# Negated scores, threshold and bias on ScalarE, and a new order of the list schedule

## The chip, the cores and the metric

One NeuronCore of one Trainium2 chip runs the whole program. The metric is the device time of one execution in microseconds (us), as a median over runs. Engines are named as in the profile: PE (TensorE matmul), PEld (its weight loads), DVE (VectorE), ACT (ScalarE), POOL (GpSimd), SP (SyncE, which only issues DMAs here).

## The reference

Attention with a thresholded softmax, then two feed-forward blocks; the first gates two projections and multiplies by `w3` and `w_out`, the second applies an ELU between `w_in` and `w_out`.

```python
# q, k, v: 4 batches x 8 heads x 576 x 64, tau = 0.02
scores = scale * np.matmul(q, k.transpose(0, 1, 3, 2))
thresh = np.max(scores, axis=-1, keepdims=True) - tau
scores = np.where(scores >= thresh, scores, -1000000000.0)
scores = scores - np.max(scores, axis=-1, keepdims=True)
attn = np.exp(scores)
attn = attn / (np.sum(attn, axis=-1, keepdims=True) + 1e-09)
attn_out = np.matmul(attn, v)
...
a = x @ w1                     # x: 2304 x 512, w1, w2: 512 x 1024
b = x @ w2
x = (a * b @ w3) @ w_out       # w3: 1024 x 1024, w_out: 1024 x 512
...
h = x @ w_in                   # 512 x 2048
g = np.where(h > 0.0, h, alpha * (np.exp(np.minimum(h, 0.0)) - 1.0))
return (g @ w_out).astype(np.float32)
```

## The kernel before

**Stages.** The program has four stages. The first is attention together with the projections `ab` of batches 0 to 2. Then come the `ab` of batch 3, the product M = w3 w_out with its use on g (tiles `m` and `x2`), and the second feed-forward block (tiles `h` and `o`).

**Attention.** The 32 heads are 16 pairs. A pair has 9 score tiles of 128 rows by 576 keys, so there are 144 tiles, numbered i in the order `SEQ`. Each passes through these steps:

- `emit_S` (PE) writes the scores to one of three PSUM buffers `s`.
- `emit_max` (DVE) writes the negated row maximum to column 0 of the small tile `st`.
- `emit_bias` and `emit_tiny` (POOL, lines 423 and 419) make from it the bias of the exponential (column 2) and the threshold (column 1).
- `emit_exp` (ACT) writes the exponentials `e`.
- `emit_mask` (DVE, line 436) compares the scores with the threshold and multiplies.

The masked tile is then transposed in one of two ways. Tiles of the DMA way are split into two fp16 halves by `emit_H` (ACT, line 443) and `emit_L` (POOL, lines 447 and 448) and transposed by `emit_T`, a DMA on SP's queue. The halves lie in one of four buffers `hl`, which is free again when its DMA has read it. Tiles of the other way are transposed on PE by `emit_X` and copied by `emit_C` (ACT, line 488), and keep their PSUM buffer `s` until that copy.

**Plain and split pairs.** Pairs 0 to 3 (`NPL`) are "plain": their 36 tiles come first, their scores are made from fp32 operands, and the softmax scale `esc` is applied in the exponential. Pairs 4 to 15 are "split": `prep_s` (POOL) first scales q by `esc`, then q and k are parted into a high and a low half, so that the scores are already scaled. `by_dma(i)` is true for 10 plain and 84 split tiles. Of split pairs, the first four tiles of pairs 4 to 9 go by PE; the rest goes by DMA.

**After a group of tiles.** A pair's tiles form two groups n (4 and 5 tiles). For each group `emit_rr` (DVE) inverts the row sums, `turn_r` (PE, line 502) and `keep_r` (ACT, line 507) turn them, and `store_r` and `load_rs` (SP) send them through DRAM. `emit_PV` (PE, lines 541 and 549) multiplies with v, `emit_xf` (DVE) normalizes, and `emit_xh` (ACT, line 566) and `emit_xl` (DVE) split the result. The `ab` units of batch b (line 591) need all groups of four pairs; a unit is 12 matmuls and its results leave through `keep_a` (ACT, line 599) or `make_g` (DVE, line 606) and `store_g` (SP, line 610).

**What sets the order.** The first stage is recorded as operations with a cost, an engine and a key, and a list scheduler (`Plan`) sorts them once, when the program is built. On every engine the instructions then run in that fixed order. `AHEAD` shifts the keys by operation and stage, `SLACK` says how far an engine may look past the earliest ready operation, and the numbers in the `op(...)` calls are the assumed durations. The order within later stages is written out by hand. The weights of the third stage are loaded by DMAs from ACT's queue (`load_w`, line 237) and converted by `conv_ops` on ACT, DVE and POOL; the first of these DMAs stands on ACT behind the last instruction of the first stage.

```python
ring["s", i] = take("s", 3, o)
re = take("e", EB, ex)             # EB = 4
rh = take("hl", HLB, hi)           # HLB = 4
```

Of the kernel before, what the change touches and what calls it, by code (L numbers as in the profile page):

```python
# [69 lines left out]

# [1306 lines left out]
```

## Time and profile before

| | us |
|---|---|
| median of 3 runs | 1003.58 |
| lowest and highest run | 1001.97, 1007.71 |
| the profiled execution | 1006.17 |
| its span, first to last instruction | 1004.4 |
| PE busy | 964.4 (96%) |
| DVE busy | 716.5 (71%) |
| POOL busy | 657.6 (65%) |
| ACT busy | 564.2 (56%) |
| mean granted PE clock | 0.993 of full speed |

Busy times are unions of what an engine had in work, over the whole span. Only the first stage, which ends at 419.41 us of the span, is ordered by the scheduler; shares of that stage are read from windows of it.

### The profile page before, as it was taken

To read this page: it belongs to the slowest core of one execution; us is meant where nothing else is said; L and a number is where in the kernel's file an instruction comes from. 1 tells how busy PE (TensorE), PEld (TensorE's weight loads), DVE (VectorE), ACT (ScalarE), POOL (GpSimd) and SP (SyncE) were. 2 spreads that over 40 slices of the span, in tenths; PEclk is the share of its full clock that TensorE was granted. 3 is DMA by queue.
4 is the path that set the end of the run, shared out by engine and by line. 5 is a ranking of instruction groups with operands and counts; after the bars stand their busy time and mean duration, and the time that the engine had idled before them with its cause. 6 is when DMAs were issued, how large, how long until landed. Compare 5 with 4: busy or idle time off the path is not lost. (4 is left out here: it accounts for less than half of the span.)

```text
span 1004.4 us, 18071 instructions
## 1 busy us (share of the span) xinstructions
PE 964.4 (96%) x6102; PEld 846.7 (84%) x6102; DVE 716.5 (71%) x1234; ACT 564.2 (56%) x1045; POOL 657.6 (65%) x849
## 2 busy tenths in 40 slices
PE   8899999989999999999999999999999999999998
PEld 5556788858888888899789999898989999899997
DVE  7887988868776677489775654789676656765563
ACT  5787778768666566355435334645555344553442
POOL 4468787868898999255322223888787576875662
PEclk9999999979999999999999999999999999999999
DMA  8446666577887967777747965731215221141201
GB/s 270 152 127 194 135 147 160 143 163 156 190 185 176 191 159 150 192 259 252 250 152 246 311 228 173 260 116 54 65 51 180 72 69 52 49 132 58 69 22 63
DMA packets 182263, 152.51 MB, mean 152 GB/s; under 512 B 119484, under 2 KB 168860, under 8 KB 177564
## 3 DMA queue, kind: packets, MB, share of 16 engines
q1 hardware_dynamic: 178060, 121.72, 44.8%
q10 hardware_dynamic: 4112, 29.66, 8.4%
q8 instruction: 48, 0.79, 0.3%
q14 instruction: 43, 0.35, 0.1%
HBM read 98.89 MB, written 24.72 MB: 123 GB/s over the span
## 5 line engine op out<-in xcount | busy, mean ns | idle before, releaser
L591 PE MATMUL ab<-x,W 128*128 128x256 f32 (+1 forms) x1536 | 227.4, 298 | 0.8 <-DVE xf L560 0.7
L1206 PE MATMUL o<-W,gg 128*128 128x512 f32 x864 | 222.9, 390 | 0.0
L591 PEld LDWEIGHTS ab<-x,W 128*128 128x128 f32 x1536 | 208.3, 188 | 8.2 <-issue 5.2
L1115 POOL TENSOR_TENSOR wi<-wr,wi 128x256 fp32r<-128x256 f32 x168 | 144.3, 871 | 65.8 <-ACT wi L1114 53.3
L1206 PEld LDWEIGHTS o<-W,gg 128*128 128x128 f32 x864 | 159.9, 188 | 21.5
L436 DVE SCALAR_TENSOR_TENSOR e<-s,st,e 128x576 f32<-128x576 f32 x144 | 115.7, 813 | 31.3 <-ACT e L430 24.8
L1194 POOL TENSOR_TENSOR gg<-th,gg 128x384 fp32r<-128x384 f32 x96 | 106.3, 1108 | 46.5 <-PE h L1246 26.4
L415 DVE TENSOR_REDUCE st<-s 128x1 f32<-128x576 f32 x144 | 107.0, 751 | 27.4 <-PE s L406 12.7
L447 POOL TENSOR_TENSOR hl<-e,hl 128x512 f16<-128x512 f32 x94 | 110.4, 1175 | 19.7 <-ACT hl L443 19.2
L1246 PE MATMUL h<-sl,wi 128*128 128x384 f32 x576 | 116.5, 338 | 2.1 <-DVE th L1276 1.2
L1188 ACT ACTIVATE et<-et 128x384 f32<-128x384 f32 x96 | 50.1, 522 | 111.9 <-DVE et L1187 111.5
L1246 PEld LDWEIGHTS h<-sl,wi 128*128 128x128 f32 x576 | 102.5, 188 | 11.2 <-DVE th L1276 2.0
L1125 PE MATMUL x<-sl,M 128*128 128x384 f32 x576 | 100.6, 336 | 1.4 <-DVE sl L242 1.4
L1125 PEld LDWEIGHTS x<-sl,M 128*128 128x128 f32 x576 | 99.8, 188 | 2.1 <-DVE sl L242 2.0
L1193 ACT ACTIVATE gg<-th 128x384 fp32r<-128x384 f32 x96 | 50.6, 527 | 76.9 <-DVE th L1191 76.5
L1276 DVE TENSOR_TENSOR th<-h,th 128x384 f32<-128x384 f32 x96 | 53.2, 554 | 56.9 <-PE h L1246 56.8
L406 PE MATMUL s<-qk 128*128 128x288 f32 x480 | 86.7, 310 | 7.1 <-DVE e L436 3.7
L430 ACT ACTIVATE e<-s,st 128x576 f32<-128x576 f32 x108 | 77.8, 736 | 27.1 <-POOL st L423 21.5
L1246 PE MATMUL h<-so,wi 128*128 128x384 f32 x432 | 87.5, 337 | 2.6 <-ACT th L1286 1.8
L1246 PEld LDWEIGHTS h<-so,wi 128*128 128x128 f32 x432 | 76.6, 188 | 10.8 <-ACT th L1286 3.9
L406 PEld LDWEIGHTS s<-qk 128*128 128x128 f32 x480 | 69.5, 192 | 17.0 <-issue 6.2
L1191 DVE SCALAR_TENSOR_TENSOR th<-et,th 128x384 f32<-128x384 f32 x96 | 71.6, 746 | 16.8 <-ACT et L1188 15.4
(112 smaller groups left out, 1539.0 us busy)
## 6 DMA issues: line engine op xcount, KB each, us to landing
wr<-wi_dr SPq DMA_DIRECT2D x168, 128.0 KB
rqk<-in_qk SPq DMA_DIRECT2D x24, 576.0 KB
raw_wo<-in_wo ACTq DMA_DIRECT2D x12, 1024.0 KB
th<-g_dr SPq DMA_DIRECT2D x48, 192.0 KB
raw_w<-in_w SPq DMA_DIRECT2D x8, 1024.0 KB
raw_w<-in_w3t ACTq DMA_DIRECT2D x8, 1024.0 KB
raw_win<-in_win ACTq DMA_DIRECT2D x8, 1024.0 KB
vr<-in_v SPq DMA_DIRECT2D x16, 320.0 KB
```

Source lines behind the costliest of these rows:

```text
L406: T.matmul(s[:, n, :HS], q, k[:, c:c + HS], start=(x == 0), stop=(x == len(ops) - 1))
L415: V.tensor_reduce(st[i][:, 0:1], sc[i][:, :, :HS], axis=AX.XY, op=ALU.max, negate=True)
L430: A.activation(et[i], sc[i][:, :, :HS], AF.Exp, bias=st[i][:, 2:3] if by_dma(i) else st[i][:, 0:1])
L436: V.scalar_tensor_tensor(et[i], sc[i][:, :, :HS], st[i][:, 1:2], et[i], op0=ALU.is_ge, op1=ALU.mult, accum_out=sm[p][:, pos:pos + 1],)
L447: G.tensor_tensor(t[:, S + 64:], e[:, :512], t[:, :512], op=ALU.subtract)
L591: T.matmul(o[:, :w], wf[:, m, wx, kt, :], x[:, xx, :], start=(kt == 0 and k == 0), stop=(kt == NK - 1 and k == 2),)
L1115: G.tensor_tensor(t[:, 1], r, f32(t[:, 0]), op=ALU.subtract)
L1125: T.matmul(o[:, :TB], M[:, f, mx, e * P:(e + 1) * P], gh[j, f][:, gx, :], start=(k == 0), stop=(k == 23),)
L1191: V.scalar_tensor_tensor(x, c["t"], -1.0, x, op0=ALU.add, op1=ALU.max)
L1194: G.tensor_tensor(h[:, 1, :], x, f32(h[:, 0, :]), op=ALU.subtract)
L1206: T.matmul(po[j, t], dst["h"][:, gx, t * P:(t + 1) * P], WO[f][:, wx, :], start=(first and k == 0), stop=(last and k == 2),)
L1246: T.matmul(o[:, :TB], w[:, wx, kt, :], bs[k][:, kt, xx, :], start=(i == 0), stop=(i == 5),)
```

## The change

Scores of split pairs are made from q scaled by `nesc` = -`esc`, so they come out negated. The row reduction of a split tile is then a minimum, its result needs no negation, the comparison is `is_le`, and the exponential takes `scale=-1.0`. `lift` holds tau in column 0 and `LNS` in column 1. One ScalarE instruction adds column 0 of `st` to one column of `lift`, or to both, and so writes the threshold and, where the tile goes by DMA, the bias. For plain tiles the two small instructions also move from POOL to ACT. Assumed durations, `SLACK` and the table `AHEAD` get new numbers, so that the whole first stage is ordered anew.

```diff
-SLACK = {"PE": 0, "DVE": 0.08, "ACT": 0.03, "POOL": 0.27, "SP": 0.09, "NEW": 0.05}
+SLACK = {"PE": 0.02, "DVE": 0.06, "ACT": 0.04, "POOL": 0.5, "SP": 0.0, "NEW": 0.05}
 AHEAD = {
-    ("emit_C", 0): 101, ("emit_C", 1): -80.5, ("emit_C", 2): 21, ("emit_H", 1): -14, ("emit_H", 2): 69.5,
...
+    ("emit_C", 0): 59.5, ("emit_C", 1): -139, ("emit_C", 2): -202, ("emit_H", 1): -201.5, ("emit_H", 2): 190.5,
...
     def prep_s(h):
-        G.tensor_scalar(raw[h][:, :S], raw[h][:, :S], esc, 0.0, op0=ALU.mult, op1=ALU.add)
+        G.tensor_scalar(raw[h][:, :S], raw[h][:, :S], nesc, 0.0, op0=ALU.mult, op1=ALU.add)
...
-        V.tensor_reduce(st[i][:, 0:1], sc[i][:, :, :HS], axis=AX.XY, op=ALU.max, negate=True)
+        plain = i < NPL * TPP
+        V.tensor_reduce(st[i][:, 0:1], sc[i][:, :, :HS], axis=AX.XY, op=ALU.max if plain else ALU.min, negate=plain)
+
+    def emit_bias(i):
+        if by_dma(i):
+            A.activation(st[i][:, 2:3], st[i][:, 0:1], AF.Identity, bias=lift[:, 1:2], scale=esc)
+        else:
+            A.activation(st[i][:, 2:3], st[i][:, 0:1], AF.Copy, scale=esc)
 
     def emit_tiny(i):
         t = st[i]
-        G.tensor_scalar(t[:, 1:2], t[:, 0:1], -1.0, add2[:, (k := int(i >= NPL * TPP)):k + 1], op0=ALU.mult, op1=ALU.add)
-
-    def emit_bias(i):
-        t = st[i]
-        G.tensor_scalar(t[:, 2:3], t[:, 0:1], esc if i < NPL * TPP else 1.0, LNS if by_dma(i) else 0.0, op0=ALU.mult, op1=ALU.add)
+        if i < NPL * TPP:
+            A.activation(t[:, 1:2], t[:, 0:1], AF.Identity, bias=drop, scale=-1.0)
+        else:
+            w = 1 + int(by_dma(i))
+            A.activation(t[:, 1:1 + w], lift[:, :w], AF.Identity, bias=t[:, 0:1])
...
-            A.activation(et[i], sc[i][:, :, :HS], AF.Exp, bias=st[i][:, 2:3] if by_dma(i) else st[i][:, 0:1])
+            A.activation(et[i], sc[i][:, :, :HS], AF.Exp, bias=st[i][:, 2:3] if by_dma(i) else st[i][:, 0:1], scale=-1.0)
...
-            op0=ALU.is_ge, op1=ALU.mult, accum_out=sm[p][:, pos:pos + 1],
+            op0=ALU.is_ge if i < NPL * TPP else ALU.is_le, op1=ALU.mult, accum_out=sm[p][:, pos:pos + 1],
...
-        bi = op(call(emit_bias, i), [mx], "POOL", 0.22, i - 10) if plain or by_dma(i) else mx
-        ty = op(call(emit_tiny, i), [mx, bi], "POOL", 0.24, i - 9)
-        ex = op(call(emit_exp, i), [bi], "ACT", 0.715 if plain else 0.625, i)
+        bi = op(call(emit_bias, i), [mx], "ACT", 0.15, i - 10) if plain else mx
+        ty = op(call(emit_tiny, i), [mx], "ACT", 0.15, i - 9)
+        bi = ty if by_dma(i) else bi
+        ex = op(call(emit_exp, i), [bi], "ACT", 0.73 if plain else 0.645, i)
```

**What the order becomes on ACT at the start of the program.** The names are tiles with their numbers: `e0` is the exponential of tile 0, `st0` its small tile, `u_w12` a weight conversion, `pt` the target of `emit_C`. Before:

```order
L428 ACTIVATE e0_179<-s0_155,st0_168,esc_113 128x576
L428 ACTIVATE e1_188<-s1_163,st1_177,esc_113 128x576
L252 ACTIVATE u_w120_201<-raw_w120_148 128x1024
L428 ACTIVATE e2_211<-s2_171,st2_193,esc_113 128x576
L488 ACTIVATE pt0_0_198<-s0_155 128x5x128
```

With the change, the same stretch of ACT:

```order
L429 ACTIVATE st0_171<-st0_171,drop_117 128x1
L424 ACTIVATE st0_171<-st0_171,esc_113 128x1
L437 ACTIVATE e0_182<-s0_158,st0_171,esc_113 128x576
L429 ACTIVATE st1_180<-st1_180,drop_117 128x1
L424 ACTIVATE st1_180<-st1_180,esc_113 128x1
L437 ACTIVATE e1_191<-s1_166,st1_180,esc_113 128x576
L253 ACTIVATE u_w120_204<-raw_w120_151 128x1024
L429 ACTIVATE st2_199<-st2_199,drop_117 128x1
L424 ACTIVATE st2_199<-st2_199,esc_113 128x1
L497 ACTIVATE pt0_0_203<-s0_158 128x5x128
L437 ACTIVATE e2_222<-s2_174,st2_199,esc_113 128x576
```

Each plain tile has two more instructions on ACT, ahead of its exponential. Over the program ACT's rows go from 1062 to 1242 and POOL's from 854 to 590.

**On SP at the end of pair 7**, tiles 67 to 71, the last before a stretch in which no `ab` unit stands on PE. `hl67` to `hl70` are what is transposed, `rd7_1` the row sums that `store_r` sends out, `g0_1_6` a result of `ab`. Before:

```order
L610 DMA g_dr_67<-g0_1_6_2586 128x2x320
L521 DMA rd7_1_2692<-rt7_1_2683 2x128 x2
L522 DMA rd7_1_2692<-rt7_1_2683 2x1x64
L476 DMA_TRANSPOSE pt7_1_2711<-hl67_2513 128x9x128
L476 DMA_TRANSPOSE pt7_1_2711<-hl68_2548 128x9x128
L476 DMA_TRANSPOSE pt7_1_2711<-hl69_2602 128x9x128
L476 DMA_TRANSPOSE pt7_1_2711<-hl70_2650 128x9x128
L527 DMA rb7_1_2774<-rd7_1_2692 64x320 x2
L474 DMA_TRANSPOSE pt7_1_2711<-hl71_2744 128x9x64 x2
```

With the change:

```order
L619 DMA g_dr_67<-g0_1_6_2575 128x2x320
L485 DMA_TRANSPOSE pt7_1_2672<-hl67_2528 128x9x128
L485 DMA_TRANSPOSE pt7_1_2672<-hl68_2549 128x9x128
L485 DMA_TRANSPOSE pt7_1_2672<-hl69_2607 128x9x128
L485 DMA_TRANSPOSE pt7_1_2672<-hl70_2629 128x9x128
L530 DMA rd7_1_2732<-rt7_1_2692 2x128 x2
L531 DMA rd7_1_2732<-rt7_1_2692 2x1x64
L483 DMA_TRANSPOSE pt7_1_2672<-hl71_2709 128x9x64 x2
L536 DMA rb7_1_2768<-rd7_1_2732 64x320 x2
```

The four transposes have moved ahead of the store of the row sums. On PE, score tiles 73 and 74 stand behind the last `ab` unit of batch 0 with the change, and stood ahead of its end before; so ten score tiles (73 to 82) instead of eight (75 to 82) lie between the last `ab` unit of batch 0 and the first of batch 1.

**On ACT at the end of the first stage.** `x15_0` and `x15_1` are the results of the last pair, `a2_0_*` the evictions of the last `ab` units of batch 2, `raw_wo10` the first weight load of the third stage. Before:

```order
L443 ACTIVATE hl143_5720<-e143_5694 128x576
L599 ACTIVATE a2_0_6_5731<-ab2_0_6_0_5700 128x256
L507 ACTIVATE rt15_1_5735<-s145_5699 5x128
L566 ACTIVATE x15_0_5793<-xf15_0_5785 128x256
L599 ACTIVATE a2_0_7_5806<-ab2_0_7_0_5781 128x256
L566 ACTIVATE x15_1_5850<-xf15_1_5848 128x320
L237 DMA raw_wo10_5895<-in_wo1 128x2048
```

With the change:

```order
L452 ACTIVATE hl143_5568<-e143_5537 128x576
L516 ACTIVATE rt15_1_5580<-s145_5559 5x128
L608 ACTIVATE a2_0_4_5598<-ab2_0_4_0_5560 128x256
L575 ACTIVATE x15_0_5636<-xf15_0_5628 128x256
L608 ACTIVATE a2_0_5_5665<-ab2_0_5_0_5643 128x256
L608 ACTIVATE a2_0_6_5698<-ab2_0_6_0_5676 128x256
L575 ACTIVATE x15_1_5734<-xf15_1_5726 128x320
L608 ACTIVATE a2_0_7_5759<-ab2_0_7_0_5740 128x256
L238 DMA raw_wo10_5814<-in_wo1 128x2048
```

More `ab` units of batch 2 now come late: on PE, three whole units (36 matmuls) stand behind the last PV of pair 15 with the change, and none did before; between the last score tile and that PV stand seven units instead of five. The first weight load now stands behind the eviction of a unit that has one more unit after it on PE.

## Rows read from the trace of the kernel before

**Rows 1.** The page, part 1: busy time, share and instructions of each engine.

```profile
PE 964.4 (96%) x6102; PEld 846.7 (84%) x6102; DVE 716.5 (71%) x1234; ACT 564.2 (56%) x1045; POOL 657.6 (65%) x849
```

**Rows 2.** Windows: length, busy us of PE, PEld, DVE, ACT, POOL, clock, DMA.

```profile
8.00:50.00 42.00, 37.63 (x286) 22.97 (x284) 36.68 (x71) 32.88 (x48) 19.50 (x38) 1.00 0.64 209
50.00:199.00 149.00, 144.94 (x1104) 113.45 (x1101) 126.17 (x261) 114.55 (x185) 118.85 (x192) 1.00 0.60 153
199.00:223.00 24.00, 20.62 (x140) 14.29 (x139) 16.92 (x37) 15.64 (x29) 15.14 (x25) 0.79 0.67 142
223.00:300.00 77.00, 73.06 (x574) 64.84 (x573) 59.76 (x127) 53.85 (x93) 66.65 (x116) 1.00 0.80 179
300.00:388.00 88.00, 82.30 (x688) 77.15 (x688) 60.15 (x136) 56.92 (x100) 78.62 (x133) 1.00 0.80 173
388.00:419.41 31.41, 27.85 (x269) 25.19 (x265) 18.79 (x45) 15.44 (x30) 19.07 (x37) 1.00 0.71 146
419.41:470.40 50.99, 50.99 (x384) 50.99 (x385) 41.77 (x45) 25.76 (x36) 23.22 (x9) 1.00 0.77 267
```

**Rows 3.** Groups by line over the span: busy and mean ns, idle before.

```profile
L419 POOL TENSOR_SCALAR st<-st,add 128x1 f32<-128x1 f32 x144 | 44.4, 309 | 14.8 <-DVE st L415 4.5 <-DVE rr L496 0.7 <-PE pv L549 0.4
L423 POOL TENSOR_SCALAR st<-st 128x1 f32<-128x1 f32 x84 | 19.2, 229 | 12.5 <-DVE st L415 5.3 <-ACT hl L443 0.6 <-DVE vst L354 0.2
L423 POOL TENSOR_SCALAR st<-st,esc 128x1 f32<-128x1 f32 x36 | 13.3, 368 | 34.9 <-DVE st L415 33.4 <-ACT e L428 0.3 <-DVE rr L496 0.3
L430 ACT ACTIVATE e<-s,st 128x576 f32<-128x576 f32 x108 | 77.8, 736 | 27.1 <-POOL st L423 21.5 <-DVE st L415 4.2 <-PE s L502 0.9
```

**Rows 4.** Groups by line of ACT, from 8 to 50 us.

```profile
L428 ACT ACTIVATE e<-s,st,esc 128x576 f32<-128x576 f32 x16 | 12.8, 825 | 7.7 <-POOL st L423 7.3
```

**Rows 5.** Timeline of ACT: start, length, instruction, idle before it.

```profile
400.13 0.25 ACT L507 ACTIVATE rt<-s 4x128 f32<-4x128 f32 x1
400.29 1.34 ACT L430 ACTIVATE e<-s,st 128x576 f32<-128x576 f32 x2
```

**Rows 6.** Timelines of DVE, POOL and ACT: the first tile.

```profile
6.82 0.76 DVE L415 TENSOR_REDUCE st<-s 128x1 f32<-128x576 f32 x1 [0.29 <-PE s L394]
...
7.77 0.26 POOL L423 TENSOR_SCALAR st<-st,esc 128x1 f32<-128x1 f32 x1 [5.21 <-DVE st L415]
...
8.07 1.71 ACT L428 ACTIVATE e<-s,st,esc 128x576 f32<-128x576 f32 x2 [5.26 <-POOL st L423]
```

**Rows 7.** Timeline of 196 to 226: SP's issues, ACT and PE.

```profile
200.59 0.38 SPq L610 DMA_DIRECT2D g_dr<-g  x1
...
202.47 6.19 SPq L476 DMA_TRANSPOSE pt<-hl  x4
...
207.00 0.68 ACT L443 ACTIVATE hl<-e 128x576 f16<-128x576 f32 x1 [2.13 <-DMA pt<-hl]
...
208.33 2.82 PE L406 MATMUL s<-qk 128*128 128x288 f32 x12 [1.68 <-ACT pt L488]
```

**Rows 8.** Waits of PE from 206 to 419.41: us in total, times, longest.

```profile
PE s L502 <- DVE st L415: 3.5, 4, 1.7
PE s L406 <- DVE e L436: 3.5, 7, 1.3
```

**Rows 9.** Timeline of PE and ACT: the end of the first stage.

```profile
409.30 0.28 PE L502 MATMUL s<-ident,rr 128*5 128x128 f32 x1 [0.67 <-DVE rr L497]
...
416.05 0.30 PE L549 MATMUL pv<-pt,v 128*64 128x320 f16 x1 [0.74 <-DMA pt<-hl]
...
419.41 51.15 PE L591 MATMUL ab<-x,W 128*128 128x320 f32 x384 [0.74 <-DVE xf L560]
...
419.40 0.83 ACTq L237 DMA_DIRECT2D raw_wo<-in_wo  x2
```

**Rows 10.** Timeline of the third stage: PE waits for an eviction of M.

```profile
494.83 5.56 PE L922 MATMUL m<-WO,w 128*128 128x512 f32 x16 [2.49 <-DVE M L932]
```

**Rows 11.** Timeline of PE around 276: a wait in the middle of the stage.

```profile
276.10 0.27 PE L502 MATMUL s<-ident,rr 128*5 128x128 f32 x1 [1.70 <-DVE st L415]
```

More of the change, by code (lines that the diff above doesn't have):

```diff
@@ new lines @@
+    ("keep_r", 0): -235, ("keep_r", 1): -313.5, ("load_plain", 0): -33.5, ("load_qk", 0): 370, ("load_rs", 0): 129,
+    ("load_rs", 1): -279.5, ("load_v", 0): -3.5, ("load_w", 0): -256.5, ("low", 0): -178, ("new_pt", 0): 145.5,
+    ("prep_h", 0): -492.5, ("prep_lk", 0): 333.5, ("prep_lq", 0): 44, ("prep_s", 0): 57.5, ("prep_v", 0): 294.5,
+    ("prep_vl", 0): 239.5, ("rest", 0): -31.5, ("run_ab", 0): 3, ("run_ab", 1): 2.5, ("run_ab", 2): 3,
+    ("sign", 0): 415.5, ("store_g", 0): -369, ("store_g", 1): -75.5, ("store_g", 2): -209.5, ("store_r", 0): 30,
@@ L69 @@
+    ("store_r", 1): -45, ("top", 0): 186.5, ("turn_r", 0): -149.5, ("turn_r", 1): -18, ("v_mean", 0): -98.5,
+    ("v_scale", 0): -76.5, ("v_sum", 0): 175.5,
 }
@@ L288, in attention_moe_moe2 @@
     tmp1 = cst.tile([P, 1], F32, name="tmp1")
-    add2 = cst.tile([P, 2], F32, name="add2")
+    nesc = cst.tile([P, 1], F32, name="nesc")
+    lift = cst.tile([P, 2], F32, name="lift")
+    drop = cst.tile([P, 1], F32, name="drop")
     ident = hp_.tile([P, P], F32, name="ident")
@@ L388, in emit_S @@
         j, t = ORDER[pos]
-        a, b = qkt[2 * p], qkt[2 * p + 1]
+        a = qkt[2 * p + j % 2]
         if p < NPL:
@@ L627, in attention_moe_moe2 @@
     V.tensor_scalar(tmp1, tau_sb, 0.0, 1e30, op0=ALU.is_lt, op1=ALU.mult)
-    V.tensor_scalar(add2[:, 1:2], tau_sb, 0.0, tmp1, op0=ALU.max, op1=ALU.add)
-    V.tensor_scalar(add2[:, 0:1], add2[:, 1:2], -(D ** 0.5), None, op0=ALU.mult)
-    V.tensor_scalar(add2[:, 1:2], add2[:, 1:2], -1.0, None, op0=ALU.mult)
+    V.tensor_scalar(lift[:, 0:1], tau_sb, 0.0, tmp1, op0=ALU.max, op1=ALU.add)
+    V.memset(lift[:, 1:2], LNS)
+    V.tensor_scalar(drop, lift[:, 0:1], -(D ** 0.5), None, op0=ALU.mult)
+    V.tensor_scalar(nesc, esc, -1.0, None, op0=ALU.mult)
     pl = Plan()
@@ L665, in attention_moe_moe2 @@
         if by_dma(i):
-            hi = op(call(emit_H, i), [mk], "ACT", 0.575, i - 1)
+            hi = op(call(emit_H, i), [mk], "ACT", 0.6, i - 1)
             rh = take("hl", HLB, hi)
-            lo = op(call(emit_L, i), [hi], "POOL", 1.42, i - 1)
+            lo = op(call(emit_L, i), [hi], "POOL", 1.44, i - 1)
             re += [mk, hi, lo]
@@ L672, in attention_moe_moe2 @@
         else:
-            xo = op(call(emit_X, i), [mk], "PE", 0.54, i - 2)
-            co = op(call(emit_C, i), [xo], "ACT", 0.59, i - 3)
+            xo = op(call(emit_X, i), [mk], "PE", 0.61, i - 2)
+            co = op(call(emit_C, i), [xo], "ACT", 0.61, i - 3)
             ring["s", i] += [xo, co]
@@ L710, in attention_moe_moe2 @@
         vh = op(call(prep_v, p), [ve], "ACT", 0.72, t0)
-        vl = op(call(prep_vl, p), [vh], "DVE", 0.8, t0, port=True)
+        vl = op(call(prep_vl, p), [vh], "DVE", 0.72, t0, port=True)
         rv += [vm, vh, vl]
@@ L729, in attention_moe_moe2 @@
             pl.after(ph, *[S_[i] for i in range(NTILE) if SEQ[i][0] == old])
-            lq = op(call(prep_lq, h), [ph], "POOL", 1.4, t0 - 11 + j)
-            lk = op(call(prep_lk, h), [ph], "POOL", 1.4, t0 - 11 + j)
+            lq = op(call(prep_lq, h), [ph], "POOL", 1.49, t0 - 11 + j)
+            lk = op(call(prep_lk, h), [ph], "POOL", 1.49, t0 - 11 + j)
             ra += [ps_, ph, lq, lk]
@@ L751, in attention_moe_moe2 @@
         i = q + 2
[L752 removed]
+        tr = op(call(turn_r, p, n, i), [r, S_[i]], "PE", 0.08, q)
         ra.append(tr)
```

42 lines of the change are left out of this document (17 added, 25 removed).

## The prediction

> **What bounds the kernel now.** I read the page's busy shares first: PE works 96% of the span, and no other engine more than 71% [rows 1]. Then I cut the span into windows. From 419.41 us on, PE is full at once (50.99 of 50.99 us), and the order behind that point is written by hand; only what lies before it is sorted anew [rows 2]. So the question is how much of the first 419.41 us PE does not use. From 8 us on its idle time is 4.37 + 4.06 + 3.38 + 3.94 + 5.70 + 3.56 = 25.0 us over the six windows, each the length less PE's busy time [rows 2]. In the third of them the granted clock is 0.79 on average; its levels are 1.0 (2.4 GHz) and 0.5 (1.2 GHz), so it ran at the lower one for about two fifths of 24 us, which cost 24 x 0.21 = 5.0 us. These 30 us are all that a better order of the same matmuls can win in the stage, and they are small pieces, none over 2 us. Which engine makes PE wait differs: from 206 us on the longest sums are for the row maximum (3.5 us) and for the mask (3.5 us), both on DVE, which itself waits for the exponential [rows 8].
>
> Loads of the other engines matter as well. From 8 to 50 us, where the plain tiles run, DVE is 87% busy, ACT 78%, POOL 46%; from 223 to 388 us POOL is 88%, DVE 73%, ACT 67% [rows 2]. The change moves work from the engine that is fullest late to one that is nearly full early.
>
> **The small instructions.** POOL loses 144 + 84 + 36 instructions, 44.4 + 19.2 + 13.3 = 76.9 us [rows 3]. ACT gains two for each of 36 plain tiles and one for each of 108 split ones, 180. The trace of before has no such ACT instruction on 128x1. The nearest is the 4x128 copy of a PSUM row: it lasts 0.25 us, and the next instruction starts 0.16 us after it [rows 5]. So one costs between 0.16 us (no pointer operand) and 0.25 us (its length): an exponential with one pointer more is 0.09 us longer, 825 against 736 ns, and the new instructions have one pointer each [rows 3, 4]. That is 180 x 0.16 = 29 us to 180 x 0.25 = 45 us. The Trainium skill ("ScalarE: Activation LUTs", What ACT_TABLE_LOAD costs) gives 186 ns plus 93 ns for each pointer operand, and 93 ns of overlap between neighbours. By that the 180 would cost an estimated 180 x 0.187 = 34 us, between the two ends; no run here shows the instruction yet.
>
> None of this is a gain or a loss by itself: POOL's time comes free beside a full PE. What counts is the chain of a tile. At the first tile the maximum ends at 7.58, POOL starts at 7.77, and the exponential starts at 8.07, 0.49 us behind the maximum, with POOL idle [rows 6]. On ACT the chain is one or two instructions of 0.16 to 0.25 us and their own hand-over, which before does not show; from 0.04 us (POOL to ACT, 8.03 to 8.07) to 0.19 us (DVE to POOL). A plain tile then needs 0.36 to 0.69 us, about the same as now. A split tile of the DMA way needs 0.20 to 0.44 us instead of at least 0.49, and above all no longer stands in POOL's queue behind long subtractions: the split exponentials waited 21.5 us for POOL's bias [rows 3].
>
> **Early: a loss.** Sixteen plain tiles pass from 8 to 50 us, 2.6 us each [rows 4]; 32 more instructions are 5.1 to 8.0 us of ACT. ACT's idle time there is 9.12 us [rows 2], so it rises to 90 to 97%, with DVE at 87% in the same chain. It fits, and 7.3 us of that idle time was spent on POOL's bias [rows 4], but two engines so full wait for each other. Lower bound 0 (the new work takes the place of that wait), upper bound 11 us (none of ACT's idle time covers it: 16 x 0.69). I take **+2 us**. From 50 to 199 us ACT has 34 us of idle time, and PE has `ab` units to fill in: 0.
>
> **The thin stretch, 199 to 223 us.** Here batch 0's `ab` is used up and batch 1 is not ready, so PE has score tiles, transposes and PVs alone. The row to look at is the split of tile 71: ACT waited 2.13 us for a buffer `hl`, until 207.00, and behind it in ACT's queue stood the copies that free PSUM, so PE stood still for 1.68 us [rows 7]. The buffer was late because the transposes were issued only at 202.47, behind the store of the row sums. In the new order they follow the store of g, issued at 200.59 for 0.38 us, so they can go some 1.5 us sooner, and the stall shrinks to a few tenths. But two more score tiles fall into the stretch, for which PE has no filling. I take **-1.5 us** of idle. The clock: PE fell to 1.2 GHz after this stall and the small ones behind it, while a single wait of 1.70 us at 276 us, with full work around it, did not bring it down [rows 2, 11]. With ten bare tiles I take it that the clock falls again: **0**; if not, -5.0 us more.
>
> **Late, 223 to 388 us.** PE's idle time is 3.94 + 5.70 = 9.64 us [rows 2]. POOL was busy for 145.3 of 165 us. Spread evenly over the 411 us of the windows, its 76.9 us are 31 us here, so it falls to about 69%; ACT gains 12 to 18 us in the same way, from 110.8 to at most 129, 78%. With POOL out of the chain, maxima and masks should be ready earlier, and PE is the only full engine left. Bounds 0 (other waits take their place) and -9.6 us (all gone). I take **-4 us**, a little under half, since waits for normalized results and evictions do not depend on POOL.
>
> **The end of the stage.** PE waited 0.67 us for the row sums, 0.74 us for the last transpose and 0.74 us for the last normalization [rows 9]. Before, five `ab` units lay between the last score tile and the last PV, now seven, and three stand behind it. A unit is at most 51.15 / 32 = 1.60 us (32 units of the wider kind), so there are about 3 us more cover for the first two waits and 4.7 us for the third. **-2.1 us**; if only the last goes, -0.7.
>
> **Third stage.** The weight loads were issued at 419.40, when the last pair's result had been taken, 0.01 us before PE began batch 3 [rows 9]. Conversions that start then end in PE's wait of 2.49 us for an eviction of M at 494.83 [rows 10]. Now the loads stand behind an eviction with one more unit after it on PE: a start 1.6 us sooner against PE, less the eviction of about 0.4 us. **-1.2 us**, and the rest of the gap stays; bounds 0 and -2.5.
>
> The sum is 2 - 1.5 + 0 - 4 - 2.1 - 1.2 = -6.8 us. The profiled execution took 1006.17 us, 1.8 more than its span and 2.6 more than the median of the runs, inside their spread. It would become 999.4, and the median 1003.58 - 6.8 = **996.8 us**.
>
> **Rivals.** (1) *The clock stays up.* With the stall of 1.68 us gone, nothing in the thin stretch is as long. Another 5.0 us: 991.8. Against it: two more bare tiles. (2) *Nothing measurable.* ACT is now what the masks wait for; the late gain falls to 1, the early loss rises to 4, and of the end only the 2.1 us is left: 4 - 1 - 2.1 - 1.2 = -0.3, 1003.3. For it: the mask already waits for the exponential, and PE is 94% busy. (3) *Slower: ACT sets the pace.* Its place is 8 to 50 us. If the idle time of ACT there stays what it is, because ACT then waits for the maximum itself where it waited for POOL, all that is added is paid: 16 x 0.69 = 11.0 us at the upper price. In the later tiles the mask then waits for ACT as it did for POOL, and that gain is 0: 11.0 - 1.5 - 2.1 - 1.2 = +6.2, 1009.8. It decides from an early loss of 9.8 us, 0.61 us a tile (the other 4.8 us and the 5 us of the border below). For it: ACT at up to 97%. Against it: the 7.3 us. The Trainium skill ("ScalarE: Activation LUTs", Rules for kernel authors) is on this side, since it sends adds and multiplies to VectorE rather than ScalarE; nothing before shows such an instruction on either engine's queue in this place, and its chance is that of this rival. (4) *The new order is worse somewhere that the rows don't show*, since every instruction of the stage has moved: part of the chance for slower.
>
> **How the numbers follow.** Runs of the kernel before lie up to 0.4% from their median, so 0.5%, 5 us, is about what a measurement can tell from no change: below 998.6 is faster, above 1008.6 slower. The forecast has 0.40, the clock that stays up 0.22, nothing measurable 0.24, slower by (3) or (4) 0.14. The forecast is 1.8 us below the border and its terms may miss by 3 together, so about 0.30 of its 0.40 count as faster, with all of rival 1 and 0.04 of rival 2: 0.56 faster, 0.30 same, 0.14 slower. The range reaches from 986 (the clock stays up and the late waits go altogether, -5.0 - 5.6 - 6.8 = -17.4) to 1005 (rival 2 with the early loss a little larger); about 0.05 lie below and 0.13 above.
>
> **What the profile after would show.** The 264 small POOL instructions are gone, ACT has 180 more of 0.25 to 0.35 us, and ACT is above 90% from 8 to 50 us. PE's idle time from 223 to 388 us is about half. The split of tile 71 no longer waits for a DMA. The three waits at the end of the stage are gone, and the gap in front of M's eviction is near 1.3 us. The end of the stage lies near 414 us. If a plain tile's small instructions and hand-overs take ACT more than 0.6 us, if fewer than 14 plain tiles pass from 8 to 50 us, or if the waits for masks grow as those for POOL vanish, the forecast is wrong.

## The result: slower by 0.8%, over half of it in stages that the change does not touch

| | before | with the change |
|---|---|---|
| median of 8 runs, us | 1002.12 | 1010.71 |
| lowest to highest | 1000.32 to 1007.71 | 1008.88 to 1014.32 |
| the profiled execution, its span | 1006.17, 1004.4 | 1010.31, 1008.1 |

The ratio is 1.0082 (95% interval 1.0056 to 1.0109), outside the half per cent that the prediction took as no change. The forecast was 996.8 us with a range of 986 to 1005: the sign was wrong and the range missed.

The profile after, part 1 of the page (it answers to [rows 1]):

```profile
PE 970.1 (96%) x6102; PEld 851.1 (84%) x6102; DVE 720.5 (71%) x1235; ACT 600.5 (60%) x1225; POOL 588.7 (58%) x585
```

POOL lost 264 instructions and 69 us, ACT gained 180 and 36 us. But PE, with the same 6102 matmuls, is busy for 5.7 us more: something made matmuls longer. The windows, with the columns of [rows 2]:

```profile
8.00:50.00 42.00, 35.42 (x265) 21.61 (x262) 36.93 (x68) 38.30 (x79) 11.49 (x6) 1.00 0.64 207
50.00:199.00 149.00, 144.78 (x1098) 112.33 (x1097) 122.99 (x254) 124.90 (x255) 88.68 (x91) 0.99 0.62 154
199.00:223.00 24.00, 21.35 (x163) 16.65 (x161) 19.54 (x42) 18.98 (x39) 13.12 (x15) 0.93 0.56 121
223.00:300.00 77.00, 72.53 (x562) 64.48 (x560) 59.42 (x126) 58.95 (x118) 55.88 (x66) 0.98 0.82 181
300.00:388.00 88.00, 81.93 (x679) 75.92 (x675) 66.60 (x144) 68.10 (x140) 68.39 (x81) 0.98 0.92 177
388.00:422.15 34.15, 32.71 (x298) 30.29 (x294) 19.41 (x43) 16.30 (x35) 12.13 (x16) 1.00 0.68 132
422.15:473.21 51.06, 51.06 (x384) 51.06 (x385) 42.36 (x44) 25.79 (x35) 23.81 (x9) 1.00 0.77 271
```

PE's idle time is 6.58 + 4.22 + 2.65 + 4.47 + 6.07 + 1.44 = 25.4 us, where it was 25.0. M starts at 473.21 instead of 470.40. From there to the end of the span it is 1008.1 - 473.21 = 534.9 us, and 534.0 before; but the 534.0 contain the gap of 2.49 us [rows 10] and a clock of 0.83 from 490 to 500 us right behind it, which the change's execution does not have. A second execution of before without either (`before_again`, below) takes 999.3 - 469.23 = 530.1 us there. The last stage shows the rest. First the `o` group of before, then windows of PE (length, busy, matmuls, clock, DMA):

```profile
L1206 PE MATMUL o<-W,gg 128*128 128x512 f32 x864 | 222.9, 390 | 0.0
```

```profile
720.00:820.00 100.00, 99.29 (x498) 1.00 0.29 91
820.00:920.00 100.00, 99.25 (x499) 1.00 0.24 76
```

The two groups `o` and `h` of the change, and the same windows:

```profile
L1217 PE MATMUL o<-W,gg 128*128 128x512 f32 x864 | 226.6, 394 | 0.0
L1257 PE MATMUL h<-sl,wi 128*128 128x384 f32 x576 | 117.4, 339 | 2.4 <-DVE th L1287 1.4 <-ACT wi L1125 0.6 <-POOL wi L1126 0.2
```

```profile
720.00:820.00 100.00, 99.30 (x493) 1.00 0.29 91
820.00:920.00 100.00, 99.32 (x492) 1.00 0.25 74
```

PE is full in both, at full clock, and yet passes 493 and 492 matmuls where before passed 498 and 499; its `o` group is busy for 226.6 us at 394 ns instead of 222.9 at 390. The order there is the one written by hand, the same in both kernels.

The small instructions came out as the prediction's rows suggested. Groups of ACT over the span, then ACT at tile 8:

```profile
L432 ACT ACTIVATE st<-lift,st 128x2 f32<-128x2 f32 (+1 forms) x108 | 30.6, 288 | 5.8 <-DVE st L418 5.0
L439 ACT ACTIVATE e<-s,st 128x576 f32<-128x576 f32 x108 | 79.2, 736 | 3.7
L452 ACT ACTIVATE hl<-e 128x576 f16<-128x576 f32 x94 | 62.6, 678 | 22.5 <-DMA pt<-hl 13.3 <-DVE e L445 9.0
L422 ACT ACTIVATE st<-st,lift,esc 128x1 f32<-128x1 f32 x10 | 3.8, 378 | 0.1
```

```profile
28.87 0.28 ACT L429 ACTIVATE st<-st,drop 128x1 f32<-128x1 f32 x1
29.05 0.28 ACT L424 ACTIVATE st<-st,esc 128x1 f32<-128x1 f32 x1
29.36 0.83 ACT L437 ACTIVATE e<-s,st,esc 128x576 f32<-128x576 f32 x1
```

One lasts 0.28 us, the next starts 0.18 us after it, and a plain tile's two with their hand-over take 29.36 - 28.87 = 0.49 us. The estimate that the prediction took from the Trainium skill ("ScalarE: Activation LUTs", What ACT_TABLE_LOAD costs), 0.187 us each, agrees. The prediction gave every new instruction one pointer; the biases of the ten plain tiles that go by DMA have two (`lift` and `esc`) and last 0.38 us. The split exponentials wait 3.7 us in all, where 27.1 were POOL's doing for the most part [rows 3].

### The profile page after: what moved, and what is told of

Read it like the earlier page. It is cut to its first block, busy times and chain, and to the rows that moved or that the text cites. A ratio compares the mean times of both kernels' runs of the same rounds, so it can differ in the third digit from the quotient of the medians.

```text
span 1008.1 us, 17816 instructions
## 1 busy us (share of the span) xinstructions
PE 970.1 (96%) x6102; PEld 851.1 (84%) x6102; DVE 720.5 (71%) x1235; ACT 600.5 (60%) x1225; POOL 588.7 (58%) x585
## 4 chain that ended last, share of the span: by engine, by line
PE 51%; DVE 4%; issue 2%; DMA 1%; ACT 1%; POOL 0%; SPq 0%; ACTq 0%; DVEq 0%; POOLq 0%
PE o L1217 17%; PE h L1257 15%; PE x L1136 9%; PE ab L600 6%; PE m L933 4%; DVE th L1202 1%; DVE et L1198 1%; DMA pt<-hl 1%; DMA x_dr<-x2s 0%; DVE th L1287 0%; POOL hl L456 0%; ACT et L1199 0%; ACT wi L1125 0%; DVE sl L1050 0%; DMA wr<-wi_dr 0%
## 5 line engine op out<-in xcount | busy, mean ns | idle before, releaser
L1217 PE MATMUL o<-W,gg 128*128 128x512 f32 x864 | 226.6, 394 | 0.0
L456 POOL TENSOR_TENSOR hl<-e,hl 128x512 f16<-128x512 f32 x94 | 112.8, 1200 | 66.2 <-ACT hl L452 61.2
```

The lines of the kernel that those rows point to most:

```text
L456: G.tensor_tensor(t[:, S + 64:], e[:, :512], t[:, :512], op=ALU.subtract)
L1217: T.matmul(po[j, t], dst["h"][:, gx, t * P:(t + 1) * P], WO[f][:, wx, :], start=(first and k == 0), stop=(last and k == 2),)
```

## The experiments

Four theories came up. Theory 1: the new order is worse. Theory 2: the load on ACT is. Theory 3: the change's constants push the tiles behind them to other SBUF addresses, and these slow TensorE. Theory 4: the slower last stage belongs to the order or to the execution.

### Operations and order apart

`ops_only` has the new operations under the old `AHEAD`, `SLACK` and durations; `table_only` the old operations under the new numbers; `plain_on_pool` is the change with the plain tiles' small instructions on POOL; `before_again` is the kernel before, profiled once more.

```diff
 # ops_only, against the change
-SLACK = {"PE": 0.02, "DVE": 0.06, "ACT": 0.04, "POOL": 0.5, "SP": 0.0, "NEW": 0.05}
+SLACK = {"PE": 0, "DVE": 0.08, "ACT": 0.03, "POOL": 0.27, "SP": 0.09, "NEW": 0.05}
...
 # table_only, against before: the change's SLACK, AHEAD and durations
 # plain_on_pool, against the change
-            A.activation(t[:, 1:2], t[:, 0:1], AF.Identity, bias=drop, scale=-1.0)
+            G.tensor_scalar(t[:, 1:2], t[:, 0:1], -1.0, drop, op0=ALU.mult, op1=ALU.add)
...
```

> The new instructions on ScalarE with the old table, slack and durations; the scheduler sorts them itself. Theory 1 (the new table's order is what costs, because PE starves in four places and its clock falls there): no slower than the kernel before, 996 to 1005 us. Theory 2 (the small instructions make ScalarE the pace of the plain tiles): at least as slow as the change, 1008 to 1015 us, with the lost time before 108 us of the span.

> The old instructions on GpSimd with the new table, slack and durations. Theory 1 (the order): slower than before, 1008 us or more, and the clock falls in several places. Theory 2 (ScalarE's load): about as before, 998 to 1006 us. A table that was searched for other durations may fit these instructions badly, so a slow result alone does not decide.

> The change, but the 72 small instructions of the plain tiles stay on GpSimd. Theory 2: tile 16 starts near 48 us as before and 4 us or more come back, 1003 to 1007 us. Theory 1: the late waits and the falls of the clock stay, 1008 to 1013 us.

> The kernel before once more, for a second profile. If the fall of the clock from 209 to 219 us in its profile belongs to every execution, it is there again and the execution takes about 1006 us. If it is there in some executions only, the clock stays up and the execution takes 1000 to 1003 us; then the profile of before showed a slow execution, and the change lost about 4 us more than the two profiles show.

Measured, against before: `ops_only` 1.0153 (1.0126 to 1.0180), `table_only` 1.0361 (1.0332 to 1.0390), `plain_on_pool` 1.0305 (1.0274 to 1.0336). Windows of 50 to 199 us, first of `ops_only`, then of `table_only`:

```profile
50.00:199.00 149.00, 141.77 (x1088) 109.39 (x1089) 125.14 (x257) 125.94 (x259) 86.14 (x88) 1.00 0.64 151
```

```profile
50.00:199.00 149.00, 135.17 (x1006) 99.54 (x1006) 113.89 (x232) 103.41 (x166) 100.73 (x165) 0.98 0.56 139
```

PE's idle time there is 7.2 and 13.8 us, against 4.1 before [rows 2] and 4.2 with the change. So each table is fitted to its own operations, and a new sort of half a change costs more than the effect that is looked for. These runs tell neither theory 1 from 2 nor what one part is worth. Their last stages do bear on theories 3 and 4: `o` is busy for 226.6 us in `ops_only` and 226.5 in `plain_on_pool`, which have the change's constants, and for 222.9 in `table_only`, which has those of before under the change's numbers. `before_again` took 1001.08 us, had a granted clock of 0.93 in the thin stretch instead of 0.79, and no gap in front of M: both belong to some executions of before only.

### The addresses

In the program's own allocation a constant tile takes a slot of 32 bytes. Before has one `add2`, the change has `nesc`, `lift` and `drop` instead: two slots more. All tiles behind them on that (left) side of SBUF start 64 bytes higher: W at 1344 instead of 1280, gg, M, and the last three wi too. The tiles on the other (right) side (x, sl, so, the first four wi) stay. `before_shift64` moves the tiles of before like that; `after_unshift` moves those of the change back; `after_shift128` moves them further; `after_again` is the change, profiled once more.

```diff
 # before_shift64, against before: the order stays the same row by row
-    add2 = cst.tile([P, 2], F32, name="add2")
+    add2 = cst.tile([P, 18], F32, name="add2")
 # after_unshift, against the change
-    nesc = cst.tile([P, 1], F32, name="nesc")
-    lift = cst.tile([P, 2], F32, name="lift")
-    drop = cst.tile([P, 1], F32, name="drop")
+    add4 = cst.tile([P, 4], F32, name="add4")
+    lift, drop, nesc = add4[:, 0:2], add4[:, 2:3], add4[:, 3:4]
 # after_shift128, against the change
-    drop = cst.tile([P, 1], F32, name="drop")
+    dropt = cst.tile([P, 17], F32, name="drop")
+    drop = dropt[:, 0:1]
```

> The kernel before with its constant add2 made 18 columns wide instead of 2. Nothing of the program changes but the addresses: every tile allocated behind add2 on that side of SBUF (W0, M, ident, spread, the inputs) lies 64 bytes higher, where the change puts them too. Theory 3 (placement: the addresses slow TensorE in the later stages, whatever the order): 1.1% fewer matmuls in 100 us of the last stage (493 instead of 498), a last-stage o matmul of 394 ns instead of 390, and 4 to 5 us more than before, a ratio of 1.004 to 1.005. Theory 4 (the slower last stage is the order's, or the execution's): 498 in 100 us, 390 ns, a ratio within 0.999 to 1.001.

> The change with its three small constants in one tile of 4 columns, so that all tiles behind lie at the addresses of before; instructions and order are the change's. Theory 3: 498 matmuls in 100 us of the last stage, 390 ns, and 4 to 5 us less than the change: a ratio to before of 1.003 to 1.004, all of it lost in the first stage, which ends 3 to 4 us later than before. Theory 4: as the change, a ratio of 1.008, 493 in 100 us.

> The change with its constant drop made 17 columns wide, so that the tiles behind lie 128 bytes higher than in before, instead of 64. Theory 3, if what counts is where an address lies within a unit of 128 bytes: as the unshifted change, 498 in 100 us, a ratio of 1.003 to 1.004. Theory 3, if every shift slows: 493 in 100 us, 1.008. Theory 4: 1.008.

> The change itself, a second execution profiled. If the four places where the clock fell in its first profile (145, 215, 280 and 335 us) belong to the order, they are there again, and the first stage again ends 3 to 4 us later than before's 418 to 419 us; if they belong to that execution, some are gone and the stage ends up to 4 us earlier. The last stage shows 493 matmuls in 100 us again by theory 3, 493 to 498 by theory 4.

`before_shift64`: 1.0068 (1.0045 to 1.0092). `after_unshift`: 0.9979 (0.9957 to 1.0000). `after_shift128`: 1.0045 (1.0023 to 1.0066). The last stage of `before_shift64`, its `o` group and its windows:

```profile
L1206 PE MATMUL o<-W,gg 128*128 128x512 f32 x864 | 226.5, 394 | 0.0
```

```profile
720.00:820.00 100.00, 99.32 (x493) 1.00 0.29 92
820.00:920.00 100.00, 99.46 (x493) 1.00 0.25 74
```

That is the change's last stage, made out of before by 64 unused bytes. Theory 3 holds and theory 4 falls. `after_again` shows 493 in the stage too, at 1006.02 us, and of the four places where the clock had fallen in the first profile (145, 215, 280 and 335 us) only that at 280. Its windows of PE:

```profile
200.00:225.00 25.00, 21.66 (x173) 1.00 0.62 130
280.00:290.00 10.00, 8.57 (x72) 0.83 0.83 179
```

### Which addresses

```diff
 # before_hop64: the last stage's pool alone (gg, three wi) 64 bytes higher
+    pad = hop.tile([P, 16], F32, name="pad")
 # before_w64: add2 [P, 18] and pad [P, 48]: W, M 64 higher, gg and wi 256
 # before_shift256, before_shift32: add2 [P, 66], add2 [P, 10]
 # before_right0, unshift_right0: the right side starts at 0 of 256 instead of 224
+    rpad = ctx.enter_context(tc.tile_pool(name="rpad", bufs=1, side="right"))
+    padr = rpad.tile([P, 56], F32, name="padr")
 # before_both32: the same, and add2 [P, 10]
 # after_both64: the change with padr [P, 48]
```

> The kernel before with an unused tile of 64 bytes at the head of the last stage's pool (and one one-column memset on GpSimd to hold it). W, M and all tiles of the first stages stay where before has them; gg and half of the wi tiles, the stationary operands of the last stage, lie 64 bytes higher. Theory 3a (what counts is where W lies, the moving operand of the o matmuls, 512 columns): as before, 498 matmuls in 100 us, o 390 ns, 864 of them busy for 222.9 us, ratio 1.000. Theory 3b (what counts is where the stationary operands lie): 493 in 100 us, 226.6 us, a ratio of 1.004 or more.

> The kernel before with add2 18 columns wide, as in the shift of 64 bytes, and an unused tile of 192 bytes at the head of the last stage's pool: W and the first stages' tiles lie 64 bytes higher, gg and wi 256 bytes higher, so that these start at a multiple of 256 bytes again as in before. Theory 3a (W): 493 matmuls in 100 us, o busy for 226.6 us, ratio 1.005 to 1.007. Theory 3b (gg and wi): 498 and 222.9 us in the last stage, ratio 1.000 to 1.003.

> The kernel before with add2 66 columns wide: all tiles behind it 256 bytes higher, at multiples of 256 bytes as in before. If the place within 256 bytes is what counts: 498 matmuls in 100 us, o 222.9 us, ratio 1.000. If any other place than that of before is slower (distance to the tiles on the other side, which don't move): 493, 226.6 us, ratio 1.004 to 1.007.

> The kernel before with add2 10 columns wide: all tiles behind it 32 bytes higher, what a single further constant of one column would do. If a start that is no multiple of 256 (or 64) bytes is what slows: 493 or fewer matmuls in 100 us, o at 226 us or more, ratio 1.004 to 1.007. If only the shift of 64 and 128 bytes does: 498, 222.9 us, 1.000.

> The kernel before with a tile of 224 bytes put first on the other side of SBUF (and one one-column memset on GpSimd to hold it). In every kernel so far all tiles of that side start at 224 within a unit of 256 bytes: x, sl, so and half of the wi tiles, which TensorE reads in ab, x, h; here they start at 0 of 256. If the rule is that an operand of TensorE should start at a multiple of 256 bytes, wherever it lies: ab, x or h matmuls get shorter as o got longer by the shifts, by up to 4 ns for each of 1008 h and 576 x matmuls, up to -6 us, a ratio of 0.994 to 0.998. If 224 of 256 was no burden, or only W and gg count: ratio 1.000, 498 matmuls in 100 us of the last stage.

> The change with its constants in one tile and the same 224 bytes on the other side: every large tile at a multiple of 256 bytes. If both the rule for the other side and the change's own -2 us hold: 4 to 8 us less than before, ratio 0.992 to 0.996, the fastest of all. If the other side doesn't count: as the change with its constants in one tile, 0.998.

> The kernel before with the tiles of both sides 32 bytes further within a unit of 256: the left ones at 32 (add2 10 columns wide), the right ones at 0 instead of 224 (a tile of 224 bytes first, with one one-column memset on GpSimd). Each of the two alone was slow, 495 and 491 matmuls in 100 us of the last stage. If what counts is how the two sides stand to each other, left less right, 32 of 256 as in before: 498, o 222.9 us, ratio 1.000. If each side has its own good place: 490 to 495, o 224 us or more, ratio 1.003 to 1.007.

> The change as it is, with its three constants in tiles of their own, and the right side moved by 64 bytes of 256 too, from 224 to 32 (a tile of 192 bytes first, with one one-column memset on GpSimd). If the sides count against each other: 498 matmuls in 100 us, o 222.9 us, and the time of the change with its constants in one tile, ratio 0.996 to 0.998. If each side has its own place: 494 or fewer, ratio 1.005 or more.

The table has where tiles start within a unit of 256 bytes, from the program's allocation; the matmuls in 720 to 820 and 820 to 920 us and the busy time of the `o` group, from each profile; and the ratio to before.

| kernel | W | gg | right side | matmuls | `o`, us | ratio (95%) |
|---|---|---|---|---|---|---|
| before | 0 | 0 | 224 | 498, 499 | 222.9 | 1 |
| before_shift256 | 0 | 0 | 224 | 498, 498 | 222.8 | 1.0010 (0.9987 to 1.0033) |
| before_shift32 | 32 | 32 | 224 | 495, 496 | 223.7 | 1.0032 (1.0008 to 1.0055) |
| before_shift64 | 64 | 64 | 224 | 493, 493 | 226.5 | 1.0068 (1.0045 to 1.0092) |
| before_w64 | 64 | 0 | 224 | 494, 495 | 226.3 | 1.0035 (1.0008 to 1.0062) |
| before_hop64 | 0 | 64 | 224 | 491, 492 | 228.5 | 1.0054 (1.0025 to 1.0083) |
| before_right0 | 0 | 0 | 0 | 491, 492 | 225.4 | 1.0032 (1.0006 to 1.0057) |
| before_both32 | 32 | 32 | 0 | 498, 498 | 222.9 | 1.0018 (0.9996 to 1.0041) |
| the change | 64 | 64 | 224 | 493, 492 | 226.6 | 1.0082 (1.0056 to 1.0109) |
| after_shift128 | 128 | 128 | 224 | 493, 493 | 225.9 | 1.0045 (1.0023 to 1.0066) |
| after_unshift | 0 | 0 | 224 | 497, 498 | 222.9 | 0.9979 (0.9957 to 1.0000) |
| unshift_right0 | 0 | 0 | 0 | 492, 492 | 225.4 | 1.0035 (1.0013 to 1.0057) |
| after_both64 | 64 | 64 | 32 | 497, 498 | 222.9 | 0.9988 (0.9965 to 1.0011) |

I had expected that operands want to start at a multiple of 256 bytes. `before_shift256` fits that, `before_right0` refutes it: there every large tile does, and the stage is as slow as with the shift. Its windows, then those of `before_both32`, where the left side starts at 32, and both sides are moved by the same 32 bytes (224 to 0 is 32 more):

```profile
720.00:820.00 100.00, 99.33 (x491) 1.00 0.29 92
820.00:920.00 100.00, 99.48 (x492) 1.00 0.25 73
```

```profile
720.00:820.00 100.00, 99.30 (x498) 1.00 0.29 90
820.00:920.00 100.00, 99.22 (x498) 1.00 0.26 77
```

Two shifts that are slow by themselves are fast together, and `after_both64` cures the change itself in the same way, without undoing anything of it. The rate shows this, and the times fit it without settling it: the interval of `before_both32` overlaps those of its two halves. What counts is how the tiles stand to each other within 256 bytes: W as gg, and both 32 above the right side. `before_hop64` and `before_w64` show that it is not one operand: either of W and gg moved alone is slow.

In `before_right0` both operands of `o` lie where before has them, and `o` is slower all the same. So there are two relations, and the end of the program, which is written by hand, parts them. After the last split of a `wi` (in `before_right0` it ends at 987.9 us) `o` and `h` matmuls still alternate for some 10 us; then come 42 `o` alone. Mean ns of an `o` between the last split and the last `h`, and in 6 us of the 42, from 3 us after their start:

| kernel | with `h` between | `o` alone |
|---|---|---|
| before | 390 | 389 |
| before_shift64 | 394 | 389 |
| before_right0 | 393 | 389 |
| before_hop64 | 396 | 395 |
| before_w64 | 394 | 391 |

The rows of the last column, without that of before:

```profile
L1206 PE MATMUL o<-W,gg 128*128 128x512 f32 x28 | 6.5, 389 | 0.0
L1209 PE MATMUL o<-W,gg 128*128 128x512 f32 x28 | 6.5, 389 | 0.0
L1208 PE MATMUL o<-W,gg 128*128 128x512 f32 x27 | 6.5, 395 | 0.0
L1208 PE MATMUL o<-W,gg 128*128 128x512 f32 x28 | 6.6, 391 | 0.0
```

W against gg slows `o` by itself. Left against right slows it only while `h` matmuls, which take operands from both sides, stand between; it is not the splits of `wi` on ACT and POOL, which have ended by then. Why it still holds for the first 2 us or so of the 42 is open.

### What the change does at the addresses of before

`after_unshift2` is `after_unshift` once more; `unshift_no_small` leaves out the 180 small instructions.

```diff
     def emit_tiny(i):
+        return
...
-            A.activation(et[i], sc[i][:, :, :HS], AF.Exp, bias=st[i][:, 2:3], scale=esc)
+            A.activation(et[i], sc[i][:, :, :HS], AF.Exp, bias=st[i][:, 0:1], scale=esc)
...
-            et[i], sc[i][:, :, :HS], st[i][:, 1:2], et[i],
+            et[i], sc[i][:, :, :HS], st[i][:, 0:1], et[i],
```

> The change with its constants in one tile once more, for a firmer size of what the change does where the addresses stay: by the earlier runs 0.998 with an interval that touches 1.000. Expected 0.996 to 1.000, last stage 498 matmuls in 100 us.

> The change with its constants in one tile, and without the 180 small ScalarE instructions: exponential and mask take the maximum itself, so threshold and bias are left out of the computation. Every other instruction and its order stay. Theory A (the late waits for masks come from the small instructions, which stand in ScalarE's queue and in each tile's chain): PE's idle time from 223 to 388 us falls from 10 to 11 us to 6 or less, and that from 8 to 50 us from 5.5 to 3 or less; 5 us or more less, ratio 0.993 or below. Theory B (they come from the new order and from the waits for transposes and masks it contains): idle time within 1.5 us of the kernel with them in both stretches, ratio 0.996 to 0.998.

`after_unshift2`: 0.9963 (0.9942 to 0.9985), with 498 and 498 matmuls in the last stage. With 0.9979 for `after_unshift` and 0.9988 for `after_both64`, the change by itself is worth 0.0012 to 0.0037 of 1005, 1.2 to 3.7 us; only the interval of `after_unshift2` lies wholly below 1. Its ratio is the lowest of the kernels that leave nothing out. `unshift_no_small`: 0.9930 (0.9906 to 0.9954). Its windows:

```profile
8.00:50.00 42.00, 36.99 (x269) 22.56 (x266) 36.30 (x67) 31.60 (x46) 10.91 (x6) 1.00 0.64 206
223.00:300.00 77.00, 73.47 (x585) 65.84 (x583) 56.41 (x123) 54.60 (x97) 56.76 (x68) 1.00 0.79 184
300.00:388.00 88.00, 81.60 (x681) 76.04 (x681) 70.45 (x151) 61.75 (x110) 69.76 (x82) 0.98 0.83 180
```

The same windows of `after_unshift2`:

```profile
8.00:50.00 42.00, 36.45 (x270) 22.07 (x266) 36.70 (x67) 37.34 (x78) 10.92 (x6) 1.00 0.64 207
223.00:300.00 77.00, 72.02 (x564) 63.93 (x563) 57.29 (x122) 59.86 (x120) 56.48 (x67) 0.98 0.81 182
300.00:388.00 88.00, 82.54 (x702) 77.29 (x701) 70.43 (x152) 69.19 (x142) 69.47 (x82) 1.00 0.84 183
```

PE's late idle time is 3.53 + 6.40 = 9.9 us without the small instructions and 4.98 + 5.46 = 10.4 with them; the early one 5.0 and 5.6. Theory A of its expectation asked for 6 and 3 at most, so the waits are for the most part not theirs. Its time came true all the same: by the two ratios the small instructions cost 0.9963 - 0.9930 = 0.0033, some 3 us, but not as waits of PE in one place. The two intervals overlap, so that size is rough. Neither theory had that in full.

## Why the prediction was wrong

**The step that failed** is in its first paragraph: "the order behind that point is written by hand; only what lies before it is sorted anew". The order behind it did stay. That its durations stay was taken from this without a word, and they did not: the new constants move the operands of every later matmul. From M's start to the end of the span `after_unshift2` takes 997.8 - 467.73 = 530.1 us and the change 534.9, so 4.8 us; `o` alone is 226.6 - 222.8 = 3.8 of them. None of the rivals had it; (4), an order that is worse somewhere unseen, gave the sign with the wrong cause. That (3) named 1009.8 us, close to the 1010.71 measured, is chance: its cause, ACT as the pace of the early tiles, did not come (below).

The 4.8 us are not the whole difference. The ratios of kernels that ran side by side lie 0.0068 apart (`before_shift64` and before) and 0.0066 (`after_shift128` and `after_unshift`), 6.6 to 6.8 us. The clock is not the reason: when span x (1 - granted clock) is taken off every run's span, the medians are 1003.0 and 997.0 us in the first pair and 1002.3 and 996.5 in the second, still 6.0 and 5.8 us apart. From M's start the two shifted kernels take 533.9 and 535.5 us instead of 530.1, which is 3.8 and 5.4 of these; the rest is open. For the change itself more is open: 1.0082 lies 0.0103 and 0.0119 above the two runs with its constants in one tile. They are of other sessions, and the median of before was 1002.12 us beside the change, 1004.73 to 1006.35 in the later ones; the second execution of the change took 1006.02 us, less than all eight above. Its two profiles have M start at 473.21 and 468.96 us, and there the clock is most of the difference: 0.83 for 10 us in four places (from 143, 212, 280 and 333 us) against one (from 280), 1.7 us each.

**Late, -4: did not come.** The idle time from 223 to 388 us went from 9.64 to 10.54 us (in the second profiles of both kernels from 8.65 to 10.00). This term was mis-sized by about 5 us. POOL was out of the chain as forecast, and the waits moved, as rival 2 had it in kind. Waits of PE in the change from 206 to 422.15 us, which answer to [rows 8]:

```profile
PE s L408 <- DVE e L445: 5.1, 6, 1.4
PE s L511 <- DVE st L418: 2.4, 3, 1.4
PE s L511 <- DVE e L445: 2.1, 1, 2.1
PE s L493 <- DVE e L445: 1.9, 3, 0.7
```

Masks were 3.5 us of it in front of score tiles and are 5.1; in front of turns of row sums they were 0.6 and are 2.1, all of it one wait. That one, the longest, step by step on ACT, then DVE, then PE:

```profile
334.35 0.69 ACT L452 ACTIVATE hl<-e 128x576 f16<-128x576 f32 x1 [0.73 <-DMA pt<-hl]
...
335.44 1.15 ACT L329 ACTIVATE qk<-rqk 128x1152 fp32r<-128x1152 f32 x1
336.49 0.73 ACT L439 ACTIVATE e<-s,st 128x576 f32<-128x576 f32 x1
```

```profile
337.32 0.82 DVE L445 SCALAR_TENSOR_TENSOR e<-s,st,e 128x576 f32<-128x576 f32 x1 [1.91 <-ACT e L439]
```

```profile
338.20 0.28 PE L511 MATMUL s<-ident,rr 128*5 128x128 f32 x1 [2.05 <-DVE e L445]
```

The exponential is late because ACT stood 0.73 us for a buffer `hl` and then ran, ahead of it, the split that needed the buffer, a small instruction of 0.28 us, an eviction and a conversion of 1.15 us, as the order says. A shorter chain does nothing for a tile that stands behind such instructions. `unshift_no_small` points the same way: without the small instructions these waits stay. That the order alone makes them is not shown by itself, since no table could be changed without a new sort.

**Early, +2: right in size.** The idle time from 8 to 50 us rose from 4.37 to 6.58 (in the second profiles from 4.15 to 5.80), with ACT at 38.30 / 42 = 91%. Rival 3, ACT as the pace with 11 us, did not come.

**Thin stretch, -1.5, and the clock, 0.** SP and ACT of the change, which answer to [rows 7]:

```profile
205.44 5.61 SPq L485 DMA_TRANSPOSE pt<-hl  x4
...
209.03 0.66 ACT L452 ACTIVATE hl<-e 128x576 f16<-128x576 f32 x1
```

The split of tile 71 no longer waits for a DMA, as forecast. The idle time fell by 0.7 us, from 3.38 to 2.65, since small waits for masks stand there instead. The clock was at 0.93 of full speed in this execution (as in the second one of before) and stayed up in `after_again` and `after_unshift2`, so rival 1 was mostly right on the place. But in all three executions it fell at 280 to 290 us, to 0.83, where both profiles of before have 1.00: 10 x 0.17 = 1.7 us are paid there.

**End of the stage, -2.1: 1.3 us by its waits.** One more row of PE of before, beside [rows 9], then PE with the change:

```profile
416.61 2.06 PE L549 MATMUL pv<-pt,v 128*64 128x320 f16 x27 [0.26 <-DMA pt<-hl]
```

```profile
414.48 0.32 PE L558 MATMUL pv<-pt,v 128*64 128x320 f16 x1 [0.24 <-DMA pt<-hl]
415.08 2.06 PE L558 MATMUL pv<-pt,v 128*64 128x320 f16 x27 [0.28 <-DMA pt<-hl]
...
422.15 51.22 PE L600 MATMUL ab<-x,W 128*128 128x320 f32 x384 [0.58 <-DVE g L615]
```

The wait for the row sums is gone, that for the last transpose fell from 0.74 + 0.26 us (the prediction left the 0.26 out) to 0.24 + 0.28. The last one, 0.74 and now 0.58, changed its name: not the normalization, but the eviction of the units that were put behind it. Together they went from 2.41 to 1.10 us; all of PE's idle time from 388 us to the end of the stage fell by 2.1, from 3.56 to 1.44.

**Third stage, -1.2: right where before has the gap.** The gap in front of M's eviction is absent from both profiles of the change, and from one of the two of before. With the shifted kernels counted in, four of the nine profiles with the order of before have 2.5 to 3.4 us of such waits, and none of the eight with the order of the change more than 0.3. So what was forecast as a gap half closed is one that no longer opens; over the nine it makes some 1.4 us a profile, near the 1.2 by chance.

With the relation of before between the tiles, the change as a whole measures -1.2 to -3.7 us, not -6.8: of its terms mostly the late one was too large.

## What to carry to other kernels

A change that adds or drops a small tile can move every tile behind it, as here; before a difference is put down to instructions, look at a stage that the change does not touch, and count the matmuls of a full window in it. An unused tile of the same size in the kernel before is the cheap control, and a table that was fitted to its operations can't be tested in halves. A chain that gets shorter wins only where the instruction that ends it is not queued behind others on the same engine.

## What the runs showed of the hardware

TensorE's rate in a full stage depended on where the tiles that it reads lie to each other within 256 bytes: 498 matmuls in 100 us at one relation, 491 to 496 at all six others that were tried, 390 against up to 396 ns for an `o` matmul. Moving both sides alike by 32 or by 64 bytes, or one side by 256, changed nothing. Where `o` had run alone for 3 us, only its own two operands still mattered: 389 ns with W and gg moved alike, 395 and 391 with one moved against the other. What in the chip does it no run here shows. The Trainium skill ("SBUF — State Buffer", A bandwidth-pool intuition that's wrong (but worth ruling out)) lists a second, independent read port for weight loads beside the moving operand's. That alone would suggest that the place of the weights does not matter to the moving operand; the measured rows differ from that, since gg moved alone gave the 395 ns.
